# Attention and two gated/squared layers on one core: another product plan for half of `wo`, weight parts at nine places, a planner with other numbers

## The chip, the cores and the metric

The kernel runs on one NeuronCore of a Trainium2 chip, as one program. Engines are named as the profile names them: PE multiplies matrices, DVE, ACT and POOL work elementwise, SP's queue issues the transfers. The metric is the device time of one execution in microseconds (us), smaller is better.

## The reference

Causal attention over 2 batches, 12 heads, 448 rows, 64 columns; its output, 896 rows by 768, goes through a normalised gated layer and then through a squared one, all in float32:

```
x  = attention(q, k, v)                          # 896 x 768
xn = x / rms(x) * rms_g
y  = (silu(xn @ w_gate) * (xn @ w_val)) @ w_out  # 768 -> 1536 -> 768
h  = max(y @ w_in, 0)                            # 768 -> 2048
return (h * h) @ w_out2                          # 2048 -> 768
```

## The kernel before

Everything is kept transposed: a tile holds 128 features of one batch, 128 partitions by 448 rows, and there are two batches. A matrix product is made of PE instructions of 128x128 stationary weights against 448 moving columns. For nearly float32 accuracy each weight and each activation is split in a high and a low part: `form` makes the two parts of up to three 128x128 weight blocks in a `ring` buffer (the high one by a rounding copy, line 267 or 265, the low one by a subtraction, line 676), `parts` does the same for a row tile in a `part` buffer (lines 267 and 559), and `product` issues three matmuls per block (high by high, high by low, low by high; line 691). Weights arrive as 64-bit numbers, and `weights` decodes a block of 768 columns with two ACT instructions (lines 639 and 644) and one or two of DVE (line 649).

Where it can, the kernel multiplies 2x2 blocks in seven products instead of eight: `halves` takes two column blocks of a weight matrix (the two rows of the 2x2 scheme are the batches, the inner halves three blocks each), forms seven weight combinations, and runs seven `product`s of nine matmuls, 63 for what a plain product does in 72. The activations' sums and differences come from `differences`, with line 723 for the differences. `seven` runs `halves` over the column pairs of a matrix, `whole` makes plain products of one column block after another. `kept` adds a product to its row tile (line 981).

The second half of `wo` (its rows 768 to 1535) is multiplied as follows before: two column pairs by `seven`, the last pair, column blocks 2 and 5, by `whole`, so with 2 blocks x 2 batches x 18 = 72 matmuls.

The order of all instructions is written by a planner, `Order.run`: each step has a due time, the engines that could do it with a duration each, and the buffers that it needs. The planner takes the step that can begin first, among those within `SLACK` the one due first, and picks the engine with the earliest end plus a price (`COST`, or `PORT` for DVE steps that share an input with POOL and are due late enough, by `EASY` and `EARLY`). Attention is twelve pairs of heads, planned `STRIDE` apart; while it runs, four blocks of weights (`ws`, into `wt` tiles) are decoded ahead for the first gated tiles, which use the attention's score banks (line 895). `norm` puts the normalisation of a batch between the pairs: sums of squares on PE (line 573) and a row of scales (line 592).

Of the kernel before, what the change touches and what calls it, by code (L numbers as in the profile page):

```python
# [8 lines left out]
F32 = mybir.dt.float32  # L9
F32R = mybir.dt.float32r  # L10
BF16 = mybir.dt.bfloat16
U32 = mybir.dt.uint32
# [5 lines left out]
B, H, S, D = 2, 12, 448, 64  # L18
DM, DF1, DF2 = 768, 1536, 2048
P = 128  # L20
CP = 64
NCH = S // CP
NCC = DM // P
NF1 = DF1 // P
NF2 = DF2 // P
NPAIR = H // 2
# [3 lines left out]
CN = 112  # L30
NE = 2
STRIDE = 5.5
SLACK = 0.1
SWITCH = 0.1
SOON = 12.0
COST = {"D": 0.4, "P": 0.4}
PORT = 1.0
EASY = 1015
EARLY = 8
LAT = {"S": 0.0}  # L40
NEXT = 0.05
SPARE = 0.15
# [12 lines left out]
class Order:  # L55
# [58 lines left out]
    def cost(self, e, t):  # L114


        if e == "D" and t["port"] and t["due"] >= max(EASY, self.now - EARLY):
            return PORT
        return COST.get(e, 0.0)

    def run(self):
# [8 lines left out]
        while open_:  # L130
# [20 lines left out]
            first = min(opt, key=lambda c: (c[1], c[2], c[3]))  # L151
            c = min((c for c in opt if c[4] == first[4] and c[1] <= first[1] + SLACK), key=lambda c: (c[2], c[3]))
            _, b, _, _, e, t, end = c
# [33 lines left out]
def tile_attention_moe_moe2(ctx: ExitStack, tc: tile.TileContext, qk, v, wg, wv, wo, w2i, w2o, rms_g, out):  # L187
# [16 lines left out]
    pw = ctx.enter_context(tc.tile_pool(name="pw", bufs=1))  # L204
# [5 lines left out]

    shapes = dict(raw=([P, 6 * P, 2], U32), wt=([P, 6 * P], F32), st=([P, 3 * P], F32), ring=([P, 6 * P + 64], F32R),
                  snap=([P, S], F32), tt=([P, S], F32), uu=([P, S], F32), part=([P, 2, S], F32R), row=([P, S], F32),
                  s=([P, 1024], F32))
    order = Order(dict(qk=3, v=3, p1=2, p2=2, pt=2))
    add, chain, buf = order.add, order.chain, order.buf

    def have(pool, **n):
        for name, k in n.items():  # L220
            for _ in range(k):
                i = len(order.places.get(name, ()))

                def make(name=name, i=i):
                    t = pool.tile(shapes[name][0], shapes[name][1], tag=f"{name}{i}", name=name, bufs=1)
                    if name == "ring":

                        o = 63
                        t = t[:, o:o + 6 * P].rearrange("p (a k n) -> p a k n", a=2, k=3)
                    return t  # L230

                order.more(name, make)

    def banks(name, *which):
        for i in which:
            order.more(name, lambda i=i: psum.tile([P, 512], F32, tag=f"b{i}", name=name, bufs=1))

    have(psum, s=2)
    banks("t", 0, 1, 2)
    banks("o", 3)  # L240
    have(pw, raw=2, wt=2, st=4, ring=8)
    have(pt_, snap=5, tt=2, uu=2, part=6, row=14)


# [35 lines left out]
    for i, fill in enumerate((1.0, -1.0e9 * float(D) ** 0.5)):  # L280
        for k in range(2):
            for sl in (slice(0, D), slice(D, P)):
                t = half[sl, 2 * i + k]
# [8 lines left out]
    for i in range(NV):  # L292
        t = atc.tile([P, 4, 2 * D], F32, name=f"vt{i}")
# [3 lines left out]
    for i in range(2):  # L297
        t = atc.tile([P, 2, 512], F32, name=f"p2t{i}")
# [251 lines left out]
    def parts(src, due, prev=(), bs=None):  # L550

        bf, t, new = src[0], src[1], [] if bs else [buf("part")]
        bs = bs or new[0]

        def high(e):
            rnd(E(e), bs.tile[:, 0], bf.tile)

        def low(e):
            E(e).tensor_sub(bs.tile[:, 1], bf.tile, bs.tile[:, 0].bitcast(F32))  # L559

        t = add(due, {"A": A_(S), "P": P_(S)}, high, [t], new=new, uses=[bf] if new else [bf, bs], prev=prev)
        return bs, add(due, {"P": P_(S, True), "D": D_(S)}, low, [t], uses=[bf, bs], port=True)
# [177 lines left out]
    def halves(a, b, f, due, done, scale=1.0, begin=0.0, home="s", sums=None, end=False):  # L740
# [36 lines left out]
        p2 = product(z, fa12, f["B21"], due + 1.8, True, True, [p1])  # L777
        k1 = snap(x, p1, due + 1.8 - SOON, 0, 0)
        done(0, 0, z, k1[0], [p2, k1[1]], due + 4 - SOON, False)
        p6 = product(x, fs2, f["T2"], due + 3.6, False, True, [k1[1]], True)  # L780
        k2 = snap(x, p6, due + 5.5 - SOON, 0, 1)
        p5 = product(y, fs1, f["T1"], due + 5.4, True, True, [p6])
        p7 = product(x, fs3, f["T3"], due + 7.3, False, True, [k2[1]], True)
        k3 = snap(x, p7, due + 9 - SOON, 1, 1)
        r = done(1, 1, y, k3[0], [p5, k3[1]], due + 9 - SOON, True)
        if end:
            sums[0][1] = k4 = snap(x, p7, due + 9 - SOON, 1, 0)
            x = buf("m")
# [9 lines left out]
    hf = [[None] * NF1, [None] * NF1]  # L798
# [107 lines left out]
        have(p, part=18, row=18)  # L906

    add(0.0, {"X": 0.0}, rows_come, used)
    norm(0, (NPAIR + 3.5) * STRIDE, 8.0)
    norm(1, 0.0, 0.3)  # L910
    ws = []
    for k in range(2 * NE):
        due = 40 + 8.0 * k
        c, t = weights((wg, wv)[k % 2][k // 2], NCC, due, due, "wt")
        ws.append([form((c, o, t), 3, due) for o in (0, 3 * P)])
    whole_tiles(0, ws, 1000.0)
# [6 lines left out]
    f = differences(xf, 1012.0)  # L923
    f.update(B11=xs[0][:3], B21=xs[0][3:], B22=xs[1][3:])
    due = 1020.0
# [36 lines left out]
    def halved(x, k0, prev=(), both=False):  # L962

        x = [y[k0:k0 + NCC] for y in x]
        f = dict(B11=[parts(x[0][j], due - 6 + j, prev) for j in range(3)],
                 B21=[parts(x[0][j + 3], due - 5 + j, prev) for j in range(3)])
        f.update(differences(x, due - 4, prev, both))
        f.update(B22=[parts(x[1][j + 3], due + j + 6, prev) for j in range(3)])
        return f

    def highs(f):
        return [x[1] for y in (f.values() if isinstance(f, dict) else f) for x in y]
# [22 lines left out]
    def seven(src, k0, f, sums, due, last=False, n=NCC // 2):  # L995


        for a in range(n):
            c = (a, a + NCC // 2)
            own = [[sums[j][c[i]] for i in range(2)] for j in range(B)]  # L1000

            def done(i, j, bank, snap, after, due, keep, c=c, own=own):
                t = kept(own, i, j, bank, snap, after, due, c[i] if last else None)
                sums[j][c[i]] = own[j][i]
                return t

            halves(src[c[0]][:, k0:k0 + NCC], src[c[1]][:, k0:k0 + NCC], f, due, done,
                   sums=own if own[0][0] else None, end=last and a == NCC // 2 - 1)
            due += 12.8
        return due  # L1010

    def whole(src, k0, n, x, sums, due, a0=0):

        for a in range(a0, NCC):
            c = a // 2 + a % 2 * NCC // 2
            layer(src[c], x, k0, [n], due, lambda b, bank, t, due, c=c: kept(sums, c, b, bank, None, [t], due))
            due += 1.22 * n * 2
        return due

    yf = [[None] * NCC, [None] * NCC]  # L1020
    g = halved(hf, 0, highs(f))
    due = seven(wo, 0, g, yf, due)
    hx = halved(hf, NCC, highs(g))
    due = seven(wo, NCC, hx, yf, due, n=NCC // 2 - 1)
    hy = [[parts(hf[1][NCC + i], due - 5 + i, highs(hx)) for i in range(3)]]
    due = whole(wo, NCC, NCC, [hx["B11"] + hx["B21"], hy[0] + hx["B22"]], yf, due, NCC - 2)
    f = halved(yf, 0, highs(hy))
    h2 = [[None] * NF2, [None] * NF2]

    def squared(b, ft, bank, snap, after, due, keep=False):  # L1030
# [28 lines left out]
    hx = split(h2, 0, 4, highs(f))  # L1059
    due = whole(w2o, 0, 4, hx, of, due)  # L1060
    f = halved(h2, 4, highs(hx), True)
    due = seven(w2o, 4, f, of, due)
    g = halved(h2, 10, highs(f))
    due = seven(w2o, 10, g, of, due, True)
# [43 lines left out]
```

## Time and profile before

| | us |
|---|---|
| median of 3 runs | 553.03 (550.48 to 555.04) |
| the profiled execution | 552.47 |
| its span, first to last instruction | 550.7 |

The span lies 1.8 us under the time of its own execution. The three runs lie 0.8% apart. In the profile, busy time of PE is drawn with modelled ends, so it says that PE had work, and the number of matmuls in a stretch says how fast it went.

### The profile page before, as it was taken

What the parts mean: (1) busy time and instruction counts of PE and PEld (TensorE: products, weight loads), DVE (VectorE), ACT (ScalarE), POOL (GpSimd) and SP (SyncE); (2) the same over time, 40 slices, a digit from 0 to 9 for tenths busy, and PEclk for the clock granted to TensorE, in tenths of its full rate; (3) what the DMA queues carried; (4) which work ended last, traced back from release to release, by engine and by line L of the source; (5) the groups of instructions that cost most, each with busy time, mean ns of one, the idle gap of its engine ahead of it and who ended that gap; (6) DMA issues with size and microseconds to landing.
All of it is one profiled execution on the core that took longest, in us unless ns stands there. A gap on an engine that the chain in (4) does not pass through costs nothing.

```text
span 550.7 us, 8919 instructions
## 1 busy us (share of the span) xinstructions
PE 540.6 (98%) x3067; PEld 477.3 (87%) x3067; DVE 420.2 (76%) x781; ACT 411.0 (75%) x879; POOL 301.8 (55%) x338
## 2 busy tenths in 40 slices
PE   8999999999999999999999999999999999999997
PEld 5776666798899999999999989899899999999996
DVE  3667867699999897889867877996777544778883
ACT  3889989656867766679888776888887998659610
POOL 3555555325232372248999789231113897899810
PEclk9999989999999999999999999999999999999999
DMA  7246514023144333333544153243332343333422
GB/s 184 86 140 191 166 55 132 0 78 130 57 147 165 116 115 115 114 116 114 170 140 149 58 174 115 62 156 128 114 117 77 114 154 114 115 115 116 148 85 83
DMA packets 19501, 65.06 MB, mean 118 GB/s; under 512 B 2048, under 2 KB 8960, under 8 KB 19456
## 3 DMA queue, kind: packets, MB, share of 16 engines
q1 hardware_dynamic: 19376, 64.27, 35.8%
q8 instruction: 24, 0.39, 0.3%
q10 hardware_dynamic: 80, 0.23, 0.1%
q14 instruction: 21, 0.17, 0.1%
HBM read 61.74 MB, written 2.75 MB: 117 GB/s over the span
## 4 chain that ended last, share of the span: by engine, by line
PE 74%; DVE 13%; ACT 6%; DMA 3%; issue 2%; POOL 1%; POOLq 0%; DVEq 0%; ACTq 0%
PE m L691 61%; DVE part L559 3%; PE t L472 3%; PE o L510 3%; PE s L359 3%; DVE ring L676 2%; DMA raw<-in_w2i 2%; PE s L372 2%; DVE row L723 1%; PE s L895 1%; ACT ring L267 1%; ACT p2t L430 1%; DVE s L649 1%; POOL p L456 1%; ACT s L639 1%
## 5 line engine op out<-in xcount | busy, mean ns | idle before, releaser
L691 PE MATMUL m<-part,ring 128*128 128x448 f32 x2115 | 429.4, 365 | 1.4 <-ACT ring L267 0.6
L691 PEld LDWEIGHTS m<-part,ring 128*128 128x128 f32 x2115 | 396.9, 188 | 33.8 <-ACT ring L267 1.2
L559 POOL TENSOR_TENSOR part<-row,part 128x448 fp32r<-128x448 f32 x103 | 121.5, 1204 | 50.6 <-ACT part L267 47.3
L676 DVE TENSOR_TENSOR ring<-s,ring 128x384 fp32r<-128x384 f32 (+1 forms) x156 | 82.3, 541 | 39.1 <-ACT ring L267 38.3
L267 ACT CAST ring<-s 128x384 fp32r<-128x384 f32 (+1 forms) x156 | 71.5, 471 | 23.8 <-PE m L691 14.8
L267 ACT CAST part<-row 128x448 fp32r<-128x448 f32 x131 | 69.1, 571 | 6.8 <-DVE row L611 2.6
L723 POOL TENSOR_TENSOR row<-row 128x448 f32<-128x448 f32 x57 | 66.3, 1179 | 12.3 <-DVE row L835 11.4
L644 ACT ACTIVATE raw<-raw 128x768 uint32<-128x768 uint8 (+1 forms) x70 | 62.5, 895 | 13.9 <-DMA raw<-in_w2o 4.5
L265 POOL TENSOR_SCALAR ring<-st 128x384 fp32r<-128x384 f32 x14 | 7.4, 527 | 100.9 <-PE m L691 48.6
L639 ACT ACTIVATE s<-raw 128x768 f32<-128x768 f32 (+1 forms) x64 | 54.0, 853 | 7.9 <-DVE ring L676 6.4
L649 DVE SCALAR_TENSOR_TENSOR s<-s,raw 128x768 uint32<-128x768 uint32 (+1 forms) x64 | 48.8, 762 | 10.9 <-ACT s L639 5.9
L676 POOL TENSOR_TENSOR ring<-st,ring 128x384 fp32r<-128x384 f32 x45 | 45.9, 1038 | 5.0 <-ACT ring L267 3.7
L456 POOL TENSOR_SCALAR p<-p,r 128x128 f32<-128x128 f32 (+1 forms) x48 | 24.0, 517 | 27.0 <-DVE r L446 25.1
L267 ACT CAST ring<-st 128x384 fp32r<-128x384 f32 x44 | 21.5, 515 | 23.0 <-DVE st L703 22.4
L405 DVE TENSOR_REDUCE mx<-s 128x2 f32<-128x256 f32 (+2 forms) x36 | 24.1, 688 | 17.9 <-PE s L375 11.2
L703 DVE TENSOR_TENSOR s<-s,st 128x384 f32<-128x384 f32 x56 | 31.6, 564 | 1.6
L456 POOL TENSOR_SCALAR p2t<-p2t,r 128x256 f32<-128x256 f32 (+1 forms) x36 | 23.1, 658 | 17.3 <-DVE r L446 7.3
L703 DVE TENSOR_TENSOR st<-st,s 128x384 f32<-128x384 f32 x56 | 30.5, 545 | 0.2
L359 PE MATMUL s<-qk 64*128 64x128 f32 (+2 forms) x144 | 26.4, 448 | 1.6 <-ACT p2t L430 1.1
L981 DVE TENSOR_TENSOR row<-m,row 128x448 f32<-128x448 f32 x36 | 22.3, 618 | 6.7 <-PE m L691 6.4
L308 ACT COPY snap<-m 128x448 f32<-128x448 f32 x43 | 22.8, 530 | 5.2 <-PE m L691 5.0
L559 DVE TENSOR_TENSOR part<-row,part 128x448 fp32r<-128x448 f32 x37 | 25.3, 708 | 0.9 <-ACT part L267 0.8
(101 smaller groups left out, 564.4 us busy)
## 6 DMA issues: line engine op xcount, KB each, us to landing
raw<-in_w2i SPq DMA_DIRECT2D x16, 768.0 KB, 4.2
raw<-in_wg SPq DMA_DIRECT2D x12, 768.0 KB, 4.5
raw<-in_wv SPq DMA_DIRECT2D x12, 768.0 KB, 4.3
raw<-in_wo SPq DMA_DIRECT2D x12, 768.0 KB, 4.3
raw<-in_w2o SPq DMA_DIRECT2D x12, 768.0 KB, 4.5
qk<-in_qk SPq DMA_DIRECT2D x11, 448.0 KB, 4.0
raw<-in_w2o SPq DMA_DIRECT2D x6, 512.0 KB, 3.7
out_t<-row SPq DMA_DIRECT2D x12, 224.0 KB, 1.9
```

The lines of the kernel that those rows point to most:

```text
L267: eng.copy(o, i)
L359: nc.tensor.matmul(s[:, h, o:o + n], z["qk"][BOTH[h], 0, qs], z["qk"][BOTH[h], 1, :n], start=True, stop=False)
L405: nc.vector.tensor_reduce(z["mx"][:, k:k + 2], src, AX, ALU.max)
L456: E(e).tensor_scalar(t, t, z["r"][:, k:k + 1], 1.0, ALU.mult, ALU.mult)
L559: E(e).tensor_sub(bs.tile[:, 1], bf.tile, bs.tile[:, 0].bitcast(F32))
L639: nc.scalar.activation(bt.tile[:, :n * P], br.tile[:, :n * P, 1].bitcast(F32), AF.Prelu, scale=2.0 ** -112, alpha=2.0 ** 32)
L644: nc.scalar.activation(br.tile[:, :n * P, 0], b, AF.Copy, scale=1.0 / 32, bias=-31.0 / 64)
L649: nc.vector.scalar_tensor_tensor(dst.tile.bitcast(U32) if dst else u, u, 3, br.tile[:, a:b, 0], ALU.logical_shift_left, ALU.bitwise_or)
L676: E(e).tensor_sub(br.tile[:, 1, :n], num(), br.tile[:, 0, :n].bitcast(F32))
L691: nc.tensor.matmul(bank.tile[:, :S], bw.tile[:, a, i], x[:, c], start=first and i == 0 and k == 0, stop=last and i == n - 1 and k == 2, sk ...
L703: (E(e).tensor_add if plus else E(e).tensor_sub)(bs.tile[:, o:o + 3 * P], x, y)
L723: E(e).tensor_sub(bs.tile, a[0].tile, b[0].tile)
```

## The change

Four things change. First, the last column pair of `wo`'s second half is multiplied by `seven` like the others, and the extra parts `hy` for the plain product go away. Second, the eight `ring` tiles, each of which began 252 bytes past a multiple of 256, become nine buffers in one tile `rings`, at 12, 28, 48, 64, 84, 92, 128, 136 and 152 bytes past a multiple of 256; the `st` tiles for weight sums go from four to three. Third, the four blocks decoded during attention are due at 26, 41, 56 and 71 where they were due at 40, 48, 56 and 64, and the first batch's normalisation moves a little. Fourth, the planner's numbers change.

```diff
-SLACK = 0.1
+SLACK = 0.15
 SWITCH = 0.1
-SOON = 12.0
-COST = {"D": 0.4, "P": 0.4}
-PORT = 1.0
-EASY = 1015
-EARLY = 8
+SOON = 14.0
+COST = {"D": 0.3, "P": 0.4}
+PORT = 1.1
+EASY = 1020
+EARLY = 5
...
-                    if name == "ring":
-
-                        o = 63
-                        t = t[:, o:o + 6 * P].rearrange("p (a k n) -> p a k n", a=2, k=3)
...
-    have(pw, raw=2, wt=2, st=4, ring=8)
+    have(pw, raw=2, wt=2, st=3)
+
+    NR = 9
+    rings = pw.tile([P, NR * 6 * P + 64], F32R, name="rings")
+    for i in range(NR):
+        o = i * 6 * P + (3, 7, 12, 16, 21, 23, 32, 34, 38)[i]
+        order.more("ring", lambda o=o: rings[:, o:o + 6 * P].rearrange("p (a k n) -> p a k n", a=2, k=3))
...
-    norm(0, (NPAIR + 3.5) * STRIDE, 8.0)
+    norm(0, (NPAIR + 4) * STRIDE, 7)
...
-        due = 40 + 8.0 * k
+        due = 26 + 15 * k
...
-    due = seven(wo, NCC, hx, yf, due, n=NCC // 2 - 1)
-    hy = [[parts(hf[1][NCC + i], due - 5 + i, highs(hx)) for i in range(3)]]
-    due = whole(wo, NCC, NCC, [hx["B11"] + hx["B21"], hy[0] + hx["B22"]], yf, due, NCC - 2)
-    f = halved(yf, 0, highs(hy))
+    due = seven(wo, NCC, hx, yf, due)
+    f = halved(yf, 0, highs(hx))
```

What this does to the order is shown at two places. The first is ACT in the middle of attention, from one pair's first exponential to the next pair's. `p` and `p2t` are the softmax tiles, `nb` the negated maxima, `pt` the transposed softmax copied from PE's bank, `raw` and `wt` the two decoding instructions, `tt` a square. Before:

```order
L430 ACTIVATE p_751,su<-s,nb 128x128
L644 ACTIVATE raw<-raw 128x768
L430 ACTIVATE p_751,su<-s,nb 128x128
L430 ACTIVATE p_751,su<-s,nb 128x384 x2
L535 ACTIVATE tt<-row 128x448
L267 CAST ring<-wt 128x384
L639 ACTIVATE wt<-raw 128x768
L410 ACTIVATE nb<-mx 128x3
L308 COPY pt<-t 128x2x4x64
L430 ACTIVATE p2t_123,su<-s,nb 128x256 x2
L430 ACTIVATE p2t_123,su<-s,nb 128x448
L308 COPY pt<-t 128x4x128
```

Now, one of the pairs that still hold a decoding:

```order
L428 ACTIVATE p_656,su<-s,nb 128x128 x2
L428 ACTIVATE p_656,su<-s,nb 128x384 x2
L533 ACTIVATE tt<-row 128x448
L642 ACTIVATE raw<-raw 128x768
L637 ACTIVATE wt<-raw 128x768
L408 ACTIVATE nb<-mx 128x3
L428 ACTIVATE p2t_126,su<-s,nb 128x256 x2
L428 ACTIVATE p2t_126,su<-s,nb 128x448
L306 COPY pt<-t 128x4x128
L408 ACTIVATE nb<-mx 128x4
```

The pair keeps its two decoding instructions, but loses two of its three copies (a third one stands behind the last row shown of before) and the rounding copy; the pairs next to it hold no decoding. Over the program ACT's `pt` copies go from 41 to 20 and DVE's from 7 to 28.

The second place is PE where `wo` ends and the first layer of the squared part begins. Each row is one block of a product, and `m` is the bank that it fills. Before, the last two plain products of `wo` and the first product of the next layer:

```order
L691 MATMUL m_3890<-part_3293,ring_3754 128x448 x3
L691 MATMUL m_3890<-part_3389,ring_3754 128x448 x3
L691 MATMUL m_3890<-part_3428,ring_3754 128x448 x3
L691 MATMUL m_3909<-part_3560,ring_3754 128x448 x3
L691 MATMUL m_3909<-part_3577,ring_3754 128x448 x3
L691 MATMUL m_3909<-part_3581,ring_3754 128x448 x3
L691 MATMUL m_3965<-part_3766,ring_3775 128x448 x3
L691 MATMUL m_3965<-part_3768,ring_3775 128x448 x3
L691 MATMUL m_3965<-part_3888,ring_3775 128x448 x3
```

Now, from the last product of `wo` (bank `m_3764`) to the first of the next layer that needs what it gave (bank `m_3798`, which got its first product from ready tiles ahead of `wo`'s last two):

```order
L689 MATMUL m_3764<-part_3483,rings_73 128x448 x3
L689 MATMUL m_3764<-part_3492,rings_73 128x448 x3
L689 MATMUL m_3764<-part_3525,rings_73 128x448 x3
L689 MATMUL m_3857<-part_3579,rings_73 128x448 x3
L689 MATMUL m_3857<-part_3597,rings_73 128x448 x3
L689 MATMUL m_3857<-part_3743,rings_73 128x448 x3
L689 MATMUL m_3875<-part_3694,rings_73 128x448 x3
L689 MATMUL m_3875<-part_3735,rings_73 128x448 x3
L689 MATMUL m_3875<-part_3851,rings_73 128x448 x3
L689 MATMUL m_3897<-part_3694,rings_73 128x448 x3
L689 MATMUL m_3897<-part_3735,rings_73 128x448 x3
L689 MATMUL m_3897<-part_3851,rings_73 128x448 x3
```

Three products of the next layer, 27 matmuls, now stand between the end of `wo` and the first product on `m_3798` again.

Elsewhere the counts move as well: of the low weight parts that read an `st` tile, DVE makes 49 where it made 13 and POOL 11 where it made 45; DVE squares 22 row tiles where it squared 9, and ACT the rest. PE has 2106 matmuls at its product line where it had 2115.

## Rows read from the trace of the kernel before

**Rows 1.** The page: the span, and busy time of four engines.

```profile
span 550.7 us, 8919 instructions
...
PE 540.6 (98%) x3067; PEld 477.3 (87%) x3067; DVE 420.2 (76%) x781; ACT 411.0 (75%) x879; POOL 301.8 (55%) x338
```

**Rows 2.** Busy time by stretch: two of attention, one with the normalisation, the gated layer.

```profile
core 0: us, PE busy (x) PEld busy (x) DVE busy (x) ACT busy (x) POOL busy (x), PEclk, DMA share, GB/s
...
14.00:38.14 24.14, 24.14 (x243) 17.27 (x241) 14.23 (x35) 20.53 (x72) 12.57 (x25) 1.00 0.29 87
38.14:67.63 29.49, 28.59 (x281) 19.75 (x280) 23.04 (x48) 27.97 (x89) 17.00 (x31) 1.00 0.59 187
67.63:78.96 11.33, 10.23 (x81) 7.25 (x81) 6.96 (x17) 9.53 (x28) 6.44 (x11) 0.85 0.30 98
...
104.00:256.80 152.80, 152.32 (x761) 141.31 (x760) 136.66 (x246) 107.92 (x198) 59.87 (x56) 1.00 0.35 114
```

**Rows 3.** PE's timeline in attention: the first score matmuls of pairs, the sums, a wait.

```profile
31.24 0.49 PE L359 MATMUL s<-qk 64*128 64x128 f32 x4
...
38.14 0.49 PE L359 MATMUL s<-qk 64*128 64x128 f32 x4
...
60.10 0.49 PE L359 MATMUL s<-qk 64*128 64x128 f32 x4
...
67.63 0.49 PE L359 MATMUL s<-qk 64*128 64x128 f32 x4
...
68.95 0.95 PE L573 MATMUL o<-ones,snap 128*112 128x1 f32 x8
71.00 0.70 PE L359 MATMUL s<-qk 64*128 64x256 f32 x4 [1.10 <-ACT p2t L430]
...
78.96 0.49 PE L359 MATMUL s<-qk 64*128 64x128 f32 x4
```

**Rows 4.** Busy time by stretch, columns as in rows 2: where the clock was down.

```profile
71.60:75.50 3.90, 3.90 (x26) 2.76 (x24) 2.55 (x3) 3.58 (x12) 3.46 (x5) 0.56 0.01 4
```

**Rows 5.** The page's groups: product matmuls and their weight loads over the whole span.

```profile
L691 PE MATMUL m<-part,ring 128*128 128x448 f32 x2115 | 429.4, 365 | 1.4 <-ACT ring L267 0.6
L691 PEld LDWEIGHTS m<-part,ring 128*128 128x128 f32 x2115 | 396.9, 188 | 33.8 <-ACT ring L267 1.2
```

**Rows 6.** PE by line from 181.5 to 256 us.

```profile
L691 PE MATMUL m<-part,ring 128*128 128x448 f32 x374 | 75.0, 363 | 0.0
```

**Rows 7.** PE by line from 388 to 494 us.

```profile
L691 PE MATMUL m<-part,ring 128*128 128x448 f32 x515 | 106.6, 370 | 0.0
```

**Rows 8.** Groups by line: the copies and low weight parts that change engines.

```profile
L676 POOL TENSOR_TENSOR ring<-st,ring 128x384 fp32r<-128x384 f32 x45 | 45.9, 1038 | 5.0 <-ACT ring L267 3.7 <-PE m L691 0.2
...
L308 ACT COPY pt<-t 128x512 f32<-128x512 f32 x41 | 23.9, 591 | 2.5 <-PE t L472 2.3
...
L676 DVE TENSOR_TENSOR ring<-st,ring 128x384 fp32r<-128x384 f32 x13 | 8.1, 650 | 0.0
...
L308 DVE COPY pt<-t 128x512 f32<-128x512 f32 x7 | 4.8, 680 | 1.1 <-PE t L472 1.1
```

**Rows 9.** Groups of the page: what follows a product of `wo` before it is multiplied again.

```profile
L559 POOL TENSOR_TENSOR part<-row,part 128x448 fp32r<-128x448 f32 x103 | 121.5, 1204 | 50.6 <-ACT part L267 47.3
...
L267 ACT CAST part<-row 128x448 fp32r<-128x448 f32 x131 | 69.1, 571 | 6.8 <-DVE row L611 2.6
L723 POOL TENSOR_TENSOR row<-row 128x448 f32<-128x448 f32 x57 | 66.3, 1179 | 12.3 <-DVE row L835 11.4
...
L981 DVE TENSOR_TENSOR row<-m,row 128x448 f32<-128x448 f32 x36 | 22.3, 618 | 6.7 <-PE m L691 6.4
```

More of the change, by code (lines that the diff above doesn't have):

```diff
@@ L209, in tile_attention_moe_moe2 @@
     atc = att.enter_context(tc.tile_pool(name="atc", bufs=1))
-    shapes = dict(raw=([P, 6 * P, 2], U32), wt=([P, 6 * P], F32), st=([P, 3 * P], F32), ring=([P, 6 * P + 64], F32R),
+    shapes = dict(raw=([P, 6 * P, 2], U32), wt=([P, 6 * P], F32), st=([P, 3 * P], F32),
                   snap=([P, S], F32), tt=([P, S], F32), uu=([P, S], F32), part=([P, 2, S], F32R), row=([P, S], F32),
@@ L222, in have @@
                 i = len(order.places.get(name, ()))
-                def make(name=name, i=i):
-                    t = pool.tile(shapes[name][0], shapes[name][1], tag=f"{name}{i}", name=name, bufs=1)
-                    if name == "ring":
-                        o = 63
-                        t = t[:, o:o + 6 * P].rearrange("p (a k n) -> p a k n", a=2, k=3)
-                    return t
-                order.more(name, make)
+                order.more(name, lambda name=name, i=i: pool.tile(shapes[name][0], shapes[name][1], tag=f"{name}{i}",
+                                                                   name=name, bufs=1))
     def banks(name, *which):
```

## Prediction, made before the changed kernel ran

> **What bounds the kernel now.** I read the page first: PE has work for 540.6 of 550.7 us, and no other engine for more than 76% of the span [rows 1]. So the time is PE's own, and three things can shorten it: fewer matmuls, a faster pace of the same matmuls, or less waiting inside PE's busy time. The list of PE by line says that the product line waits only 1.4 us in the whole span [rows 5], so little is left to win from waits behind attention.
>
> The same list, cut to two stretches without a wait, shows that the pace is not one number: 374 matmuls in 75.0 us, 200.5 ns each, and 515 matmuls in 106.6 us, 207.0 ns each [rows 6, 7]. Instructions, shape and granted clock (1.00) are the same in both, and in both every weight part began 252 bytes past a multiple of 256. So PE has at least two paces at one and the same place of the weights, and keeps one for long. The other 1,600 or so product matmuls run near 200.5, so the mean is about (515 x 207.0 + 1672 x 200.5) / 2187 = 202.0 ns.
>
> In attention the windows show two regimes. From 14 to 38 us ACT is busy for 20.53 of 24.14 us, and from 38 to 68 us for 27.97 of 29.49 us [rows 2]: the second is the stretch in which the four weight blocks are decoded. The timeline of PE shows what this does: a pair takes 38.14 - 31.24 = 6.90 us while ACT has room, then (60.10 - 38.14) / 3 = 7.32 and 67.63 - 60.10 = 7.53 us [rows 3]. Then PE waits 1.10 us for an exponential of ACT [rows 3], right behind the sums of one column each, and after that the granted clock is 0.56 over 3.9 us [rows 4]: some 3.4 of them at 1.2 GHz, the rest at 2.4.
>
> **The change part by part.** *Seven products for the last pair of wo.* 72 matmuls become 63. Nine matmuls of 200.5 ns are 1.80 us, of 207.0 ns 1.86 [rows 6, 7]; I take 1.8. It removes three `parts` on ACT and POOL or DVE and adds weight sums on DVE, all off PE's path as long as the next layer finds its operands. That is the exposure of this part: the last product of `wo` now finishes a tile that goes through a sum, two differences, a rounding and a low part before a product of the next layer can read it. With POOL doing what it can this chain is 0.62 + 1.18 + 1.18 + 0.57 + 1.20 = 4.75 us [rows 9]. The changed order puts 27 matmuls, 27 x 0.2005 = 5.4 us, between the last product of `wo` and the first that needs the tile. So I cost it at nothing, with 0 to 1 us in the range for hand-overs between engines that the chain doesn't hold. The three plain products that closed `wo` before hid the same chain in the same way.
>
> *Decoding spread, copies to DVE.* The two decoding instructions of ACT stay, but they alternate with pairs that have none, and 21 `pt` copies go from ACT (0.591 us each) to DVE (0.680) [rows 8]. In 38 to 68 us four pairs kept ACT busy for 27.97 us, 7.0 each [rows 2]. A pair with a decoding now loses two copies (1.2 us), which leaves 5.8, and one without loses more; 5.8 is under the 6.90 us that PE needs for a pair. So ACT stops being the bound there. What that gives back at most: 3 x 0.42 + 0.63 = 1.9 us from the four long pairs, 1.1 us from the wait at 71.00, and half of the 3.4 us at the low clock, 1.7 us, if the fall goes with the wait that stands ahead of it. Together 4.7 us. At least it gives nothing, or a loss: DVE was busy for 23.04 of 29.49 us there, 5.76 in a pair [rows 2]; one more copy in most pairs and half a low weight part (0.68 + 0.3) make 6.7, of 6.90. DVE then has the place that ACT has now, with the maxima and reciprocals of the softmax queued behind its copies and decodings, and PE's scores and POOL's scaling waiting for those. Between the ends I take 2.8 us, 60% of the most, nearer to the row of the first stretch (ACT at 85%, pairs of 6.90) than to that of the second.
>
> *Low weight parts from POOL to DVE.* 36 more on DVE at 0.650 us, 34 fewer on POOL at 1.038 [rows 8]. That is 23.4 us more for DVE, and with the copies (14.3) and 13 squares (8, if one takes the 0.618 us of an elementwise step of this shape [rows 9]) DVE comes to about 420 + 46 = 466 us of 550, and ACT and POOL fall. In the gated layer, where DVE is fullest, it has 136.66 of 152.80 us [rows 2]; a third of the moved parts there is 7.8 us, so 144.5 of 152.8. It still has room, and the products wait 1.4 us in all [rows 5], so I take 0, with -0.5 to +2 us for the range. The ninth ring lets parts stand ready a product earlier (1.8 us), which works in the same direction as the other 0.5.
>
> *Nine places for the weight parts.* No row shows a place other than 252, so the trace bounds this from both sides only by its two paces. All 2178 product matmuls at 200.5 ns would be 2178 x 1.5 ns = 3.3 us less than now, all at 207.0 ns 2178 x 5.0 ns = 10.9 us more. A gain beyond 3.3 us isn't excluded either: the load of the weights takes 188 ns [rows 5], and if that were the pace, it would be 2178 x 14 ns = 30.5 us less. I take 0, the present mix, because both paces occur at one place, so the place can't be the only cause, and nothing tells which way another place pulls.
>
> The Trainium skill would have the places do nothing: SBUF — State Buffer, section Who interferes with whom, gives PE two read ports of its own, one for the moving operand and one for the weights, and says that PE never waits on anyone; by that rule this part is 0, and the two paces of the trace stay unexplained, so it doesn't settle the matter. The Trainium skill also has a formula against both paces, in TensorE: Matmul & The Clock Gate, section Back-to-back issue gap: the columns over 2.4 GHz plus 2.5 ns, an estimate of 189.2 ns here; the rows disagree with it by 11 and 18 ns, nine matmuls would be 1.7 us instead of 1.8, and a place that brought PE there would give 28 us, which is the second rival.
>
> The sum is -1.8 - 2.8 + 0 + 0 = -4.6 us, from the profiled execution's 552.47 to **548 us**. Against the median of 553.03 this is -0.9%, and about 1%, 5.5 us, is what a measurement of this kernel can tell from no change, since three runs lay 0.8% apart.
>
> **The rivals.** *The places lock PE at 207 ns* (slower). The nine places differ in every product, so a phase between weight load and moving stream is set anew each nine matmuls, and the pace may settle at 207. For it: that pace exists and held for 515 matmuls. Against it: with one place PE mostly ran at 200.5. Price 10.9 us: 552.5 - 4.6 + 10.9 = 558.8. It decides against the change from a mean pace of 202.0 + 4.6 / 2178 = 204.1 ns on.
>
> *The places speed PE up.* If variety or a better start removed as much as the longer pace adds, 6.5 ns under 200.5, the pace would be 194, and the time 548 - 2178 x 8 ns = 530; half of that step gives 537. For it: a weight load alone takes 188 ns. Against it: 374 matmuls on end keep 200.5 [rows 6], so it looks like a floor.
>
> *DVE takes ACT's place in attention, and the products' gain is all there is.* DVE at 6.7 of 6.90 us in a pair has no room for the order in which its inputs come; then the long pairs stay, the wait and the low clock come at another place, and the time is 552.5 - 1.8 = 550.7, or up to 553 with 2 us of waits for DVE in the gated layer.
>
> **How the numbers follow.** The forecast, 545 to 550 with 548 as its middle, gets 0.47; DVE in ACT's place, 550 to 553, 0.25; the places that speed PE up, 530 to 541, 0.13; those that lock it at 207 ns, 554 to 560, 0.15. A range of 541 to 557 us leaves out most of the first kind of places and the upper part of the second, some 0.18. Faster by over 1% means under 547.5: the places that speed PE up (0.13), and 0.2 of the forecast's 0.47, so 0.33. Slower by over 1% means over 558.6, the upper half of the places at 207 ns: 0.08. Within 1% is the rest, 0.59.
>
> **What would show it.** In the profile after: 2106 matmuls at the product line. Attention pairs at 6.90 us between 38 and 68 us, with ACT under 90% in them; no half clock between 70 and 80 us, or one without a wait ahead of it. The end of the twelfth pair 2 to 4 us earlier. No wait over 0.5 us at the border of `wo` and the next layer. DVE near 466 us busy. And the pace: stretches without a wait at 200 to 207 ns; one number outside, or a mixture that changes from product to product, would show the places at work. The forecast is wrong if the mean pace is under 199 or over 204 ns, since each nanosecond is 2.2 us, or if waits for DVE show up at the scores.

## The result, and the profile after

The changed kernel takes 556.02 us in the median of 18 executions (554.07 to 561.16), the kernel before 548.82 us in as many (544.87 to 555.04). The ratio is 1.0131, 95% interval 1.0109 to 1.0154: 1.3% slower, where 0.9% faster was predicted. Ratios here leave out executions more than 1.5% above the fastest of their kernel; medians hold them all. The profiled execution took 555.48 us with a span of 553.6, so it lies 0.5 us under its median; the one of before, with 552.47, lay 3.65 us over what 18 executions give.

The page of the kernel after, with the lines that answer to [rows 1, 5]:

```profile
span 553.6 us, 8904 instructions
...
PE 540.6 (98%) x3058; PEld 473.7 (86%) x3058; DVE 457.2 (83%) x849; ACT 391.7 (71%) x842; POOL 262.4 (47%) x302
...
L689 PE MATMUL m<-part,rings 128*128 128x448 f32 x2106 | 431.1, 366 | 4.2 <-DVE row L808 1.5
...
L674 DVE TENSOR_TENSOR rings<-st,rings 128x384 fp32r<-128x384 f32 x49 | 32.3, 691 | 0.0
```

Nine product matmuls fewer, and yet PE is busy for the same 540.6 us: each of them takes longer. And the product line waits for 4.2 us instead of 1.4.

PE by line in the two stretches of [rows 6, 7], 181.5 to 256 us and 388 to 494 us:

```profile
L689 PE MATMUL m<-part,rings 128*128 128x448 f32 x368 | 75.1, 365 | 0.0
L689 PE MATMUL m<-part,rings 128*128 128x448 f32 x521 | 106.6, 366 | 0.0
```

368 matmuls in 75.1 us are 204.1 ns each, 521 in 106.6 are 204.6. Before it was 200.5 in the one stretch and 207.0 in the other; now there is one mixture everywhere. From start to start of neighbouring product matmuls in the trace, without the steps over 240 ns that hold a wait, the mean over the program is 203.75 ns, against 201.74 before. This measure is called the mean pace below; it covers the 72 matmuls of the first gated tiles (L895 before, L893 now) as well.

The waits of PE from 104 us on (engine and line, releaser: us in total, times, longest):

```profile
PE m L689 <- DVE row L808: 1.5, 1, 1.5
PE m L689 <- ACT snap L306: 1.3, 1, 1.3
PE m L689 <- DVE row L1030: 0.5, 1, 0.5
PE m L689 <- DVE part L557: 0.4, 1, 0.4
PE m L689 <- DVE row L764: 0.4, 1, 0.4
```

Four of the five are releases by DVE. The longest stands at 146.5 us, where DVE's queue had no gap: the row that PE needed began at 145.79 us, behind three steps of 0.55 to 0.61 us. Earlier in that same gapless queue, from 128 to 139 us, three low row parts (L557) took 1.05 to 1.58 us instead of 0.62, together 2.2 us more; whether the wait hangs on them was not tested. The wait of 1.3 us, at 272.7 us, comes after two low weight parts that took 2.94 us together from 266.18 us on.

Attention, busy time by stretch as in [rows 2], and PE's timeline as in [rows 3]:

```profile
core 0: us, PE busy (x) PEld busy (x) DVE busy (x) ACT busy (x) POOL busy (x), PEclk, DMA share, GB/s
...
38.14:67.63 29.49, 28.49 (x284) 19.87 (x281) 23.14 (x54) 25.91 (x84) 16.51 (x33) 1.00 0.46 143
67.63:78.96 11.33, 11.21 (x108) 7.93 (x104) 9.68 (x20) 9.45 (x31) 6.23 (x11) 1.00 0.46 150
```

```profile
38.40 0.49 PE L357 MATMUL s<-qk 64*128 64x128 f32 x4
...
45.73 0.49 PE L357 MATMUL s<-qk 64*128 64x128 f32 x4
...
53.06 0.49 PE L357 MATMUL s<-qk 64*128 64x128 f32 x4
...
60.21 0.49 PE L357 MATMUL s<-qk 64*128 64x128 f32 x4
...
61.96 0.92 PE L571 MATMUL o<-ones,snap 128*112 128x1 f32 x8 [0.36 <-DVE snap L538]
...
68.72 0.49 PE L357 MATMUL s<-qk 64*128 64x128 f32 x4
...
75.62 0.49 PE L357 MATMUL s<-qk 64*128 64x128 f32 x4
...
99.34 1.69 PE L508 MATMUL o<-pt,vt 128*64 128x320 f32 x16
```

The eleventh pair starts at 75.62 us instead of 78.96, the last values at 99.34 instead of 102.36, 3.0 us earlier. But by then PE had done 18 of the 72 matmuls of the first gated tiles (L895) before, and only 12 now (L893); six matmuls are 1.2 us. On equal work, up to the first matmul of the product line, behind all 72, attention gave 116.48 - 114.84 = 1.6 us (before, then now):

```profile
116.48 1.76 PE L691 MATMUL m<-part,ring 128*128 128x448 f32 x8
```

```profile
114.84 1.39 PE L689 MATMUL m<-part,rings 128*128 128x448 f32 x6
```

The pairs between 38 and 60 us still take 7.33, 7.33 and 7.15 us. ACT is at 88% there and DVE at 78%, and the 6.90 us that were expected don't come. What is gone is the wait of 1.10 us and the stretch at half the clock (a mean granted clock of 0.85 there in [rows 2], 1.00 now). What that clock costs by itself is seen in an execution of the old order with the weights at 192 bytes (an experiment below): it has the same wait, 1.11 us, but the full clock, and this pair took 9.71 us in place of 11.33.

```profile
65.69:75.40 9.71, 8.60 (x81) 6.15 (x80) 7.16 (x17) 9.35 (x28) 6.45 (x11) 1.00 0.34 108
```

So against the profiled execution of before, split at the first matmul of the product line: -1.6 (attention), -1.8 (nine matmuls), +2106 x 2.0 ns = +4.2 (pace), +2.2 (what the steps over 240 ns, those with a wait, took beyond the pace; the idle times of the page give 2.8) = +3.0 us, where the span grew by 2.9.

### The profile page after: what moved, and what is told of

Same layout as the page of the kernel before. It is cut to its first block, busy times and chain, and to the rows that moved or that the text cites. A ratio compares the mean times of both kernels' runs of the same rounds, so it can differ in the third digit from the quotient of the medians.

```text
span 553.6 us, 8904 instructions
## 1 busy us (share of the span) xinstructions
PE 540.6 (98%) x3058; PEld 473.7 (86%) x3058; DVE 457.2 (83%) x849; ACT 391.7 (71%) x842; POOL 262.4 (47%) x302
## 4 chain that ended last, share of the span: by engine, by line
PE 79%; DVE 15%; issue 2%; ACT 2%; POOL 2%; DMA 1%; POOLq 0%; DVEq 0%; ACTq 0%
PE m L689 65%; PE o L508 3%; PE t L470 3%; DVE part L557 3%; PE s L357 3%; DVE rings L674 3%; PE s L370 2%; DVE row L721 1%; PE s L893 1%; POOL p L454 1%; DVE mx L403 1%; PE o L503 1%; DMA qk<-in_qk 1%; DVE st L701 1%; DVE s L647 1%
## 5 line engine op out<-in xcount | busy, mean ns | idle before, releaser
L689 PE MATMUL m<-part,rings 128*128 128x448 f32 x2106 | 431.1, 366 | 4.2 <-DVE row L808 1.5
L689 PEld LDWEIGHTS m<-part,rings 128*128 128x128 f32 x2106 | 394.4, 188 | 40.8 <-ACT snap L306 1.9
L557 POOL TENSOR_TENSOR part<-row,part 128x448 fp32r<-128x448 f32 x100 | 117.4, 1198 | 50.0 <-ACT part L265 48.5
L674 DVE TENSOR_TENSOR rings<-s,rings 128x384 fp32r<-128x384 f32 (+1 forms) x157 | 82.2, 541 | 22.7 <-ACT rings L265 21.7
L265 ACT CAST rings<-s 128x384 fp32r<-128x384 f32 (+1 forms) x157 | 70.0, 477 | 16.0 <-DVE s L647 5.3
L721 POOL TENSOR_TENSOR row<-row 128x448 f32<-128x448 f32 x57 | 69.3, 1234 | 20.3 <-DVE row L833 18.6
L263 POOL TENSOR_SCALAR rings<-st 128x384 fp32r<-128x384 f32 x12 | 6.2, 515 | 113.9 <-DVE st L701 77.9
L265 ACT CAST rings<-st 128x384 fp32r<-128x384 f32 x48 | 23.1, 515 | 26.2 <-DVE st L701 18.7
L674 DVE TENSOR_TENSOR rings<-st,rings 128x384 fp32r<-128x384 f32 x49 | 32.3, 691 | 0.0
L557 DVE TENSOR_TENSOR part<-row,part 128x448 fp32r<-128x448 f32 x37 | 27.8, 767 | 0.7 <-ACT part L265 0.6
```

The source lines that it names most:

```text
L265: eng.copy(o, i)
L674: E(e).tensor_sub(br.tile[:, 1, :n], num(), br.tile[:, 0, :n].bitcast(F32))
L689: nc.tensor.matmul(bank.tile[:, :S], bw.tile[:, a, i], x[:, c], start=first and i == 0 and k == 0, stop=last and i == n - 1 and k == 2, sk ...
L721: E(e).tensor_sub(bs.tile, a[0].tile, b[0].tile)
```

## The experiments

Two theories stood behind the first runs. *Places*: every place of the stationary weights has a pace, a mixture of nine has the mean of them, and 252 is one of the best. *DVE*: the planner's numbers gave DVE more than it can take in time, and PE waits for it. The rival to both was that seven products or the spread decoding bring the loss.

The runs came in sets on different chips, each with the kernel before beside it. Its median was 550.76 us beside one place, eight places, the dues of before and the planner of before at one place; 548.70 beside the planner of before at nine places, the sums on POOL, the plain products and 64 bytes; 548.78 beside the two kernels at 192 bytes. Between sets, ratios are compared and not times.

**One place again, the planner as after.**

```diff
-        o = i * 6 * P + (3, 7, 12, 16, 21, 23, 32, 34, 38)[i]
+        o = i * 6 * P + 63
```

> The changed kernel with all nine buffers of weight parts at 252 bytes past a multiple of 256 and nothing else undone. Theory A, the places set the pace: the product matmuls come at 200 ns (207 in stretches) in place of 203.7 all along, 2178 x 3.7 ns = 8 us less, so 547 to 549 us and within 1% of the kernel before. Theory B, the planner's numbers do it through waits: the pace stays at 203 to 204 ns or its change is worth under 2 us, and the time stays at 554 or more.

Measured: median 556.2 us where before had 550.76. Of twelve executions six took 550.5 to 554.3 and six 558.2 to 561.6; the ratio is 1.0065 (1.0026 to 1.0104), that of the medians 1.010. The profiled execution, 558.15 us, is one of the long ones; none of the shorter six was traced. Its mean pace is 200.66 ns, as the theory of places has it: 3.1 ns under after, 6.7 us. In this execution the time didn't follow, and the waits show why, so each theory got one half right:

```profile
PE m L689 <- DVE row L764: 3.7, 2, 3.5
PE m L689 <- ACT snap L306: 2.0, 2, 1.8
PE m L689 <- DVE row L808: 1.5, 1, 1.5
```

The longest of them, in the timeline of the kernel with one place (start, duration, then engine, line and count):

```profile
301.62 7.81 POOL L557 TENSOR_TENSOR part<-row,part 128x448 fp32r<-128x448 f32 x7
...
303.67 0.61 DVE L979 TENSOR_TENSOR row<-m,snap 128x448 f32<-128x448 f32 x1
...
304.20 0.56 DVE L701 TENSOR_TENSOR s<-s,st 128x384 f32<-128x384 f32 x1
...
304.66 5.18 DVE L674 TENSOR_TENSOR rings<-st,rings 128x384 fp32r<-128x384 f32 x1
...
309.77 0.61 DVE L764 TENSOR_TENSOR row<-m,row 128x448 f32<-128x448 f32 x1
...
310.43 7.82 PE L689 MATMUL m<-part,rings 128*128 128x448 f32 x25 [3.46 <-DVE row L764]
```

One low weight part took 5.18 us on DVE instead of 0.55. It began while POOL worked through a row of seven low row parts without a gap, and it ended 0.4 us after the last of them. The row sum behind it (L764) came late, and PE stood for 3.46 us. DVE steps with an operand in PE's banks (`m`, `s`) kept their 0.6 us beside the same POOL steps. All low weight parts of this kernel by their input (tile, count: minimum/median/maximum ns) say the same:

```profile
L674 DVE TENSOR_TENSOR rings<-s,rings x157: 275/548/560, 135.0 to 538.6; 128x384 fp32r<-128x384 f32 x151, 128x128 fp32r<-128x128 f32 x6
L674 DVE TENSOR_TENSOR rings<-st,rings x49: 543/553/5183, 122.8 to 535.4; 128x384 fp32r<-128x384 f32 x49
L674 DVE TENSOR_TENSOR rings<-wt,rings x11: 529/550/561, 35.3 to 128.0; 128x384 fp32r<-128x384 f32 x11
```

`s` is one of PE's banks, `st` and `wt` are SBUF tiles: same instruction, same shape, at most 560 ns with one SBUF input and up to 5183 with two (the eleven that read `wt` met no hold-up here). That is what the Trainium skill says in SBUF — State Buffer, section Who interferes with whom: a DVE instruction with two SBUF inputs contends with a GpSimd (POOL) instruction that reads SBUF, by an exclusive lock. The trace agrees. That DVE's step got no turn between POOL instructions that follow each other without a gap is shown by this row, and by one more below (plain products).

The waits had a second price, the clock (windows as above):

```profile
268.00:280.00 12.00, 10.19 (x43) 9.04 (x42) 9.65 (x19) 8.77 (x16) 5.99 (x7) 0.86 0.40 132
306.00:320.00 14.00, 10.54 (x40) 9.27 (x40) 10.89 (x14) 5.93 (x11) 4.59 (x5) 0.76 0.16 51
```

Mean granted clocks of 0.86 and 0.76 mean stretches at 1.2 GHz behind waits of 1.81 and 3.46 us: 12 x 0.14 + 14 x 0.24 = 5.0 us of PE's full speed. With 4.6 us more waits than after, and 6.7 us less by the pace, that gives +2.9 us; the span grew by 2.6.

**The planner's numbers of before, at one place and at nine.**

```diff
-SLACK = 0.15
+SLACK = 0.1
...
-SOON = 14.0
-COST = {"D": 0.3, "P": 0.4}
-PORT = 1.1
-EASY = 1020
-EARLY = 5
+SOON = 12.0
+COST = {"D": 0.4, "P": 0.4}
+PORT = 1.0
+EASY = 1015
+EARLY = 8
```

At one place (with the edit above):

> The changed kernel with all buffers at 252 bytes and the planner's six numbers of before (SLACK, SOON, COST, PORT, EASY, EARLY); seven products, nine buffers, three sums' tiles and the spread decoding stay. If the waits of 4 us in the gated and later layers come from the planner's numbers, which moved low weight parts to DVE, this is 2 to 4 us faster than the run with one place alone and 1% faster than the kernel before. Rival: the waits come from having three tiles for sums or from the seven products, and it equals the run with one place alone within 1 us.

Measured 549.25 us, ratio 0.9973 (0.9944 to 1.0003): by the medians 7 us under the kernel with one place and the new numbers, more than expected. Against before the expected 1% is 0.3%, not told apart from nothing. Only 11 low parts of sums stand on DVE, none over 569 ns; PE waits 3.3 us at the product line.

At nine places:

> The changed kernel, nine places kept, with the planner's six numbers of before. If the costs of places and planner add up, the places cost 3.7 ns x 2178 = 8 us over the run with one place and these numbers (549.3), so 557, no better than the changed kernel. If the longer pace covers waits for the other engines, the waits of 3 us at the product line of that run vanish, and it is 553 to 555 us.

Measured 553.39 us, ratio 1.0097 (1.0067 to 1.0127), waits at the product line 1.4 us. Against after's 1.0131 that is 0.3%, some 2 us, though the intervals overlap; the waits of 4.2 us in after and 1.4 here have the same sign and size. So the planner's numbers cost 5 to 7 us while the matmuls are short, and some 2 while they are long. The likely reason, argued and not shown: with 3.5 ns more per matmul PE comes later to what it would have waited for. In the other direction the two kernels with the planner of before tell the places' price, 1.0097 to 0.9973, 1.2% or 7 us by the ratios (4.1 by the times, from two sets); the paces, 203.67 and 200.13 ns, give 7.7, less 1.9 of waits that the longer one hides.

**Eight places in the kernel before**, nothing else changed.

```diff
-                        o = 63
+                        o = (3, 7, 12, 16, 21, 23, 32, 34)[i]
```

> The kernel before with its eight buffers at 12, 28, 48, 64, 84, 92, 128 and 136 bytes past a multiple of 256 in place of 252, same order of instructions. Theory A: a mixed pace of 203 to 204 ns in every stretch, 2187 x 3.7 ns = 8 us more, 556 to 558 us. Theory B: the time of the kernel before, 548 to 550 us.

Measured 553.31 us, ratio 1.0040 (1.0020 to 1.0060): the time rose by 2.2 us (1.1 to 3.3) where the theory of places named 8. The mean pace is the one it named, 203.81 ns, in the two stretches:

```profile
L691 PE MATMUL m<-part,ring 128*128 128x448 f32 x367 | 75.0, 366 | 0.0
L691 PE MATMUL m<-part,ring 128*128 128x448 f32 x522 | 106.5, 366 | 0.0
```

So the pace of after (368 and 521) comes from the places alone. Between the two profiled executions the span grew by only 0.4 us: 2115 x 2.05 ns = +4.3 by the pace, -2.2 from the steps that hold a wait, -1.7 up to the first matmul of the product line (114.77 against 116.48 us). Why the medians lie no further apart than 2.2 us comes up again under the base, below.

**Low weight parts of sums only on POOL**, one place, planner as after.

```diff
-        return br, n, add(due, {**({"P": P_(w, True)} if sb else {}), "D": D_(w)}, low, [t], uses=[b, br], port=sb)
+        return br, n, add(due, {"P": P_(w, True)} if b.pool == "st" else {**({"P": P_(w, True)} if sb else {}), "D": D_(w)}, low, [t], uses=[b, br], port=sb)
```

> The changed kernel with one place (252 bytes) and all low parts of the weight sums (60, those that read an st tile) on POOL, planner's numbers as changed. Theory A: these low parts, which read two tiles of SBUF, are what costs time on DVE, by their 0.69 us each and by waiting for POOL's steps (one took 5.18 us beside five of POOL's). Then no low part on DVE lasts over 1.6 us, PE's waits at the product line fall from 8.8 to under 4 us, and the time from 556.2 to 549 to 551 us. Rival: the planner's numbers cost by the order that they make, whoever does the low parts, and the time stays over 554.

Measured 550.66 us, ratio 1.0040 (1.0010 to 1.0069). The time is where the theory put it, and under the rival's 554. But of the 5.5 us between this median and that of the kernel with one place, 2.1 are the difference of before in the two sets; some 3.4 us are left (0.4% over before instead of 1.0%), and the intervals of the two ratios overlap. What is plain is that the long group is gone: all twelve executions lie under 553.4 us, where six of twelve took 558.2 and more. The details are a partial miss. The product line still waits 4.8 us, and one DVE step (a low row part, also with two SBUF inputs) took 2.09 us. What went is the wait of 3.46 us and with it the low clock:

```profile
306.00:320.00 14.00, 14.00 (x72) 12.95 (x71) 13.36 (x25) 8.64 (x16) 8.92 (x9) 1.00 0.34 113
```

In those 14 us DVE is busier than with the long step, 13.36 us, and PE waits for nothing: being full did not hurt here, being held up did. These low parts aren't the whole price of the planner's numbers, though. The kernel is still 0.7% over the one with one place and the planner of before (0.9973, the intervals don't overlap); its profiled execution has a pace of 201.02 ns against 200.13 (1.9 us) and 4.8 us of waits against 3.3. What in the plan makes these was not tested.

**The dues of before**, all else as after.

```diff
-    norm(0, (NPAIR + 4) * STRIDE, 7)
+    norm(0, (NPAIR + 3.5) * STRIDE, 8.0)
...
-        due = 26 + 15 * k
+        due = 40 + 8.0 * k
```

> The changed kernel with the decoding due at 40, 48, 56 and 64 and the first normalisation as before; nine places and all else as changed. If the spread decoding is worth what the two traces show (the last values product starts 3 us earlier after the change), this is 2 to 4 us slower than the changed kernel, 558 to 560 us. Rival: the copies on DVE did it, which come from the planner's price and stay here, and the time stays within 1 us of 556.

Measured 557.89 us, 1.0125 (1.0090 to 1.0161): 1.9 us over after's median, nothing by the ratios. In the trace the last values are 2.4 us later than after's, and the first matmul of the product line, on equal work, 1.3 us (116.17 against 114.84 us). A gain of 0 to 1.9 us is as close as this comes; it bears out neither the 2 to 4 us expected nor the rival.

**Plain products for the last pair of `wo` again**, all else as after.

```diff
-    due = seven(wo, NCC, hx, yf, due)
-    f = halved(yf, 0, highs(hx))
+    due = seven(wo, NCC, hx, yf, due, n=NCC // 2 - 1)
+    hy = [[parts(hf[1][NCC + i], due - 5 + i, highs(hx)) for i in range(3)]]
+    due = whole(wo, NCC, NCC, [hx["B11"] + hx["B21"], hy[0] + hx["B22"]], yf, due, NCC - 2)
+    f = halved(yf, 0, highs(hy))
```

> The changed kernel with the last pair of wo's second half by plain products again, nine places and the planner's numbers as changed. Nine matmuls more at 203.7 ns are 1.8 us: 557 to 558.5 us, if seven products are worth their matmuls. Rival: the chain from the last product to the next layer costs as much as the nine matmuls save, then it equals the changed kernel within 1 us.

Measured 556.9 us, 1.0159 (1.0126 to 1.0191): 0.3% over after's 1.0131, 1.5 us, but the intervals overlap, so it isn't told apart from nothing. In this kernel, with its nine places, a low part of a sum took 4.14 us at 304.2 us beside a row of six POOL steps, so the hold-up isn't bound to one place.

**Places by themselves, in the kernel before.** All eight buffers lie at 64 bytes (`o = 16`), or all at 192 (`o = 48`):

> The kernel before with all eight buffers at 64 bytes past a multiple of 256 in place of 252. Theory A1, mixing the places sets the 203.7 ns: one place locks PE, at 200 or 207 ns, and the time is that of the kernel before within 1 us or a share of 207 ns stretches apart. Theory A2, each place has a pace of its own (64 bytes showed 202.2 ns on average among the nine): one constant pace other than 200 and 207, and for 202.2 ns a time of 552 us or so.

> The kernel before with all eight weight-part buffers 192 bytes past a multiple of 256 instead of 252, and nothing else changed. The theory that each place has a pace of its own: where eight places were mixed, the products read from 192 went at 200.1 ns in the mean, some of them at 196 to 199, so alone this place gives one pace over the whole program, between 199 and 201 ns. Against the kernel before (201.7 ns in the mean of its profiled execution) that is 0.7 to 2.7 ns by 2187 matmuls, 1.5 to 5.9 us less: a ratio of 0.989 to 0.998. The rival, that the low values at 192 came from the neighbouring products at other places (the change from one place to the next): alone it goes at 202 to 206 ns like most places, and the ratio is 1.000 to 1.017.

Measured 551.17 us and 1.0049 (1.0023 to 1.0075) at 64; 547.96 us and 0.9987 (0.9963 to 1.0011) at 192, where the expected gain is not told apart from nothing. The two stretches, first at 64, then at 192:

```profile
L691 PE MATMUL m<-part,ring 128*128 128x448 f32 x370 | 75.0, 364 | 0.0
L691 PE MATMUL m<-part,ring 128*128 128x448 f32 x526 | 106.5, 364 | 0.0
```

```profile
L691 PE MATMUL m<-part,ring 128*128 128x448 f32 x373 | 74.9, 362 | 0.0
L691 PE MATMUL m<-part,ring 128*128 128x448 f32 x532 | 106.6, 362 | 0.0
```

Each place alone has one mean through the whole program: 202.24 and 200.04 ns. Where nine were mixed, the matmuls that read from 64 had 202.2 (each product matmul in the trace, in order, put beside the address of its weights in the program). For these two the pace belongs to the place and hardly to its neighbours.

At 252 bytes it is otherwise, in all four traces that have this place alone. Beside 200.0 ns it holds two longer paces, 203.3 and 206.7 ns from start to start. Counted over nine steps at a time, of some 2,110, before has 517 steps at 207 (from 386.5 to 495 us) and 27 at 203; one place 122 and 68; one place with the planner of before 19 and none; the sums on POOL none and 555. Every such stretch begins right behind a step out of rhythm, of 212 to 1126 ns. Other breaks of this kind are followed by 200.0, and no break at 192 or 64 bytes leads to a lasting longer pace. What decides which pace follows is open.

Two runs with eight places each, 4 to 64 bytes apart, one execution each:

```diff
-                        o = 63
+                        o = (0, 8, 24, 40, 48, 52, 56, 60)[i]
```

> The kernel before with its eight buffers at 0, 32, 96, 160, 192, 208, 224 and 240 bytes past a multiple of 256. If each place has a pace of its own, as 64 bytes did alone (202.2 ns, the same as its mean among the nine), the matmuls of each buffer give a mean that differs from the others' by whole nanoseconds; places under 200 ns would be a faster choice. Rival: the mean of a buffer depends on its neighbours in time, and all eight lie within 1 ns of each other.

```diff
-                        o = 63
+                        o = (63, 62, 61, 59, 55, 51, 47, 43)[i]
```

> The same with 252, 248, 244, 236, 220, 204, 188 and 172 bytes. If the pace belongs to the place, the buffer at 252 bytes stands near 200 ns (or 207 in stretches) among slower ones; if it belongs to having one place, the buffer at 252 runs near 203.7 like the rest.

551.87 and 553.85 us, where before took 550.04 beside them; mean paces 203.51 and 203.56 ns. By place the means of the first run from 200.1 (192 bytes) and 202.1 (96) to 205.3 (160) and 206.3 (224), those of the second from 201.5 (252) and 202.0 (248) to 204.8 (236), for steps within a product; with the step to the next product counted too, the ends of the first run are 200.6 and 205.8. Four bytes beside 252 cost 0.5 ns, 28 bytes beside it (224, in the first run) 4.8. 252 itself had 200.1 alone, so a mixture moves a place's pace too, by 1.4 ns here. No rule for which place is good came out of it. The Trainium skill's sentence that PE never waits on anyone, in SBUF — State Buffer, section SBUF: two separate sides (the prediction puts it under the section Who interferes with whom), speaks of waiting for other engines. The paces here differ by up to 6 ns with the place of PE's own weights, and it says nothing of that.

**The best of the parts together**: the changed kernel with the planner of before and all nine buffers at 192.

```diff
-        o = i * 6 * P + (3, 7, 12, 16, 21, 23, 32, 34, 38)[i]
+        o = i * 6 * P + 48
```

> The changed kernel with the planner's numbers of before and all nine buffers at 192 bytes: what the runs so far point to as the fastest, if 192 is at least as good a place as 252. With all nine at 252 the same order had 200.1 ns and 0.9973 of the time before. The theory of a pace for each place: 199 to 201 ns here too, so -1.1 to +1 ns by 2178 matmuls from that, -2.4 to +2 us, about 547 to 551 where before has 549 to 551, a ratio of 0.993 to 1.001; the waits at the product line stay at 2 to 4 us. The rival (the pace came from neighbours): 202 to 206 ns, 4 to 13 us over the one at 252, a ratio of 1.005 to 1.02.

Measured 547.77 us, ratio 0.9962 (0.9935 to 0.9988): faster than before by 0.4%, and than after by 1.7%. The pace is 200.03 ns, PE waits 3.1 us at the product line. Seven products, spread decoding and the ninth buffer are in it; the places and the planner's numbers are not.

## Why the prediction was wrong, step by step

**Nine places**: "I take 0, the present mix, because both paces occur at one place, so the place can't be the only cause, and nothing tells which way another place pulls". This failed, and it is the largest term. It measured +2178 x 2.01 ns = +4.4 us against the profiled execution, inside the bounds of -3.3 to +10.9. By the times of the run that changes only the places it is +2.2 us (1.1 to 3.3), between the two kernels with the planner of before 4 to 7. The step from "not the only cause" to zero was wrong: 252 ran near its shorter pace for three quarters of the program, of the places measured only 192 came as near to 200 ns, and a mixture of nine takes their mean. The rival that locks PE at 207 ns had the sign and named the price per nanosecond, but no stretch locked: a mixture came. Its turning point, 204.1 ns, was not reached, 203.75 was; it was counted with 4.6 us of gains, of which the traces show 3.4, and it took the next term to make the kernel slower.

**Low weight parts from POOL to DVE**: "so I take 0, with -0.5 to +2 us for the range". This failed too. DVE came to 457 us as worked out (466), with 142.3 of 152.8 in the gated layer (144.5), and had room by that. But the 36 parts that moved read two SBUF tiles. The 49 on DVE now have a mean of 691 ns with a median of 553, and the waits at the product line grew by 2.8 us; with short matmuls the planner's numbers as a whole cost 5 to 7 us, by the medians about half of it through these parts. That the hold-up makes PE wait is shown at one place, where it took 3.46 us. In the changed kernel only the wait of 1.3 us stands directly behind held-up low weight parts; for the one of 1.5 us, behind a full queue, it is not shown. Busy shares can't show a hold-up, the operands can: where a step's inputs lie and how long a row of POOL's steps runs beside it. The parts of `st` on DVE before had a maximum of 1054 ns, and one difference there (L723, two SBUF inputs too) took 2100, which were the signs to go by. The rival with DVE in ACT's place had named 2 us of waits for DVE in the gated layer; waits for DVE came, there and behind it.

**Decoding spread**: -2.8 forecast, -1.6 in the two profiled executions on equal work. The step that failed is the first term of its 4.7: with ACT at 88% the pairs should have fallen to 6.90 us, and they stayed at 7.15 to 7.33. The wait at 71 us and the low clock went, as the step said they might, and the clock alone is worth the 1.6 us. How much of that is the spread is open. The order of before reaches the first matmul of the product line between 112.9 and 116.5 us in its six traces, and the profiled execution of before is the latest of them; after's attention (four traces) 113.6 to 114.8; the spread with the planner of before (three) 116.1 to 117.8. What the executions do show is the clock. Of the executions of before beside the experiments, 50 of 75 had a mean granted clock of 0.997 or less, and so had 27 of 36 of the three runs of twelve that only move its places. It was 2 of after's 18, 4 of 30 with the planner of before, and none of six with the dues of before. In the three sets such executions of before were 1.6 to 3.6 us longer in the median.

**Seven products**: -1.8 forecast; nine matmuls fewer, and 1.5 us between the kernels with and without, not told apart from nothing. No wait of 0.5 us stands at the border of `wo`, as forecast.

**The base**: the sum was made against 552.47 us, which lay 3.65 over the median of 18. The kernel before was at its longer pace for 515 matmuls in that execution. (The two paces of the prediction, 200.5 and 207.0 ns, are 200.0 and 206.7 from start to start.) Its usual pace can only be worked out, and not in one way. At 192 bytes, 200.04 ns on the whole, it is 0.7 us (-0.6 to +2.0) faster than before on the same chip, which makes about 200.4 ns. The run with eight places, 203.81 ns, rose by 2.2 us with 2.2 us less of waits, which makes about 201.8. From there to 203.75 are 7.3 or 4.2 us. With -1.8, +2.2 and 0 to -1.6 for attention this makes +3.0 to +7.7, and 7.2 were measured, so the longer waits and paces cover the loss only at the upper end. That 556.02 us lies inside the 541 to 557 that were named is luck of the base: with the base 3.65 us lower the whole range moves under it.

## What to carry to other kernels

Before elementwise work is moved to an engine that has room, look at where its operands lie: a DVE step with two SBUF inputs can be held by a row of POOL steps for as long as that row lasts (seen twice here), and what counts then is what stands behind it in DVE's queue. The place of the stationary operand is a parameter of its own; measure a place alone by matmuls per stretch without a wait, in several stretches, since one place (252) held three paces, and take the best one for all buffers, since a mixture gets the mean. And a longer pace hides waits: parts of a change that each look harmless together can each cost several microseconds when the other is taken away, so both orders want a run.

## What the runs showed of the hardware

The same 128x128 by 448 matmul stream, at the full granted clock and without waits, has mean paces of 200.0 ns (weights 192 bytes past a multiple of 256), 200.1 to 201.7 (252), 202.2 (64), 203.5 to 203.8 (eight or nine places mixed) and up to 206.3 (224, among others): 3% by the address of the weights. At 252 it held 200.0, 203.3 or 206.7 ns for long stretches, each of the longer ones begun by a break in the rhythm, with 19 to 555 matmuls off 200.0 in the four traces; at 192 none were. What sets the pace is open. A DVE subtraction of 0.55 us took 5.18 us beside seven POOL steps in a row, and the 3.46 us that PE stood for it were followed by a stretch at 1.2 GHz.
